# Decode attention over 65536 keys: keys transposed in place, one value tile split unevenly over its partitions, scores copied in pairs, one store for seven heads

## The chip, the core and the metric

The kernel runs on one core of one Trainium2 chip. The metric is the device time of one execution in microseconds (us); the time of a kernel is the median of its runs. A profile is one further execution with the hardware profiler on; its instructions cover a span that is a little shorter than the execution's time.

## The reference

One query token with 32 heads attends to 65536 keys. Eight key-value heads serve four query heads each; a head is 128 wide. All data are bf16.

```
B, Hq, Hkv, Sq, Sk, D = 1, 32, 8, 1, 65536, 128
q: (B, Hq, Sq, D)   k, v: (B, Hkv, Sk, D)

k = jnp.repeat(k, rep, axis=1); v = jnp.repeat(v, rep, axis=1)      # rep = 4
scores = jnp.einsum("bhqd,bhkd->bhqk", q, k) * D ** -0.5
p = softmax(scores, axis=-1)
return jnp.einsum("bhqk,bhkd->bhqd", p, v)
```

Keys and values are 268 MB and each of them is used once.

## The kernel before, in words

A key-value head ("group" g, eight of them) has its 65536 rows laid over 128 partitions, 512 rows each. The rows come in four tiles s = 0..3 of 128 rows per partition: 128 x 128 x 128 bf16, 4 MB in one transfer, 32 KB for each partition. Key tiles `kn` and value tiles `vb` share one pool of four buffers (`iopool`, tag "io"). All loads go through the queue of SyncE (SP) in program order: while group g's keys are loaded, the values of group g-1 are loaded between them, so that from the second group on the order is k(g,0), v(g-1,0), k(g,1), v(g-1,1) and so on, and the last four loads are v(7,0) to v(7,3). A load is issued when its buffer is free.

`k_step` takes a key tile. The contraction runs over the head's 128 dimensions, so they have to be on partitions: VectorE transposes 32 x 32 blocks of bf16 pairs taken as fp32, two of the eight row classes w at a time, from `kn` into a tile `T` (pool `tpool`, three buffers). That is four transposes of 128 x 2048 fp32 for each key tile (L135). TensorE then does four matmuls for each w (L144), all 32 of a tile summed in one PSUM bank `sc` (three buffers); `wq` holds the queries, shifted so that each w writes rows of its own. ScalarE copies `sc` to its quarter of `S_g` (L151).

After four tiles `softmax` finds the maximum (VectorE, TensorE), and ScalarE computes the exponentials with their sums (`E_g`, L177). `transpose_weights` (L190) turns them for use as weights; it is placed in the middle of the first key tile of the next group.

`v_stream` multiplies a value tile by the weights with 32 matmuls (L213) into `psum_o`, `pick` masks and adds four parts (L224, L230), and `finish` divides by the sums and calls `store`, which writes heads 0 to 3 during group 4's pass and heads 4 to 6 during group 7's (L250, on ScalarE's queue).

The last tile v(7,3) is loaded in pieces of 64, 32, 16, 8, 4 and 4 rows. `finish_last` streams the first 64 rows like every tile, and takes the rest in an order written out by hand (`manual_schedule`): transposed matmuls for rows 64 to 119 (L290), the part from `pick` in between (L287), single rows 120 to 123 (L280), a transpose (L297), single rows 124 to 127, then two VectorE operations and the store of head 7 (L305).

Everything else is ordered by the framework, which sets the semaphores. Transfers of SP's and ScalarE's queues take eight completion semaphores in turn, so a transfer's issue waits until the eighth transfer before it has landed.

Of the kernel before, what the change touches and what calls it, by code (L numbers as in the profile page):

```python
# [8 lines left out]
ALU = mybir.AluOpType  # L9
# [3 lines left out]

NT = 128
NW = 16

LATE = (64, 120, 124)

# [2 lines left out]
def kernel(  # L21
# [17 lines left out]
    nc = tc.nc  # L39
    P = nc.NUM_PARTITIONS  # L40
    B, Hq, Sq, D = q.shape
    _, Hkv, Sk, _ = k.shape
    assert B == 1 and Sq == 1 and D == P
    HPG = Hq // Hkv
    assert HPG == 4 and HPG * Hkv == Hq
    R = Sk // P
    KT = R // NT
    W = NT // NW
    assert W * HPG == 32 and KT == 4
    SCALE = float(D) ** -0.5  # L50

    fp32 = mybir.dt.float32
    bf16 = mybir.dt.bfloat16

    const = ctx.enter_context(tc.tile_pool(name="const", bufs=1))
    iopool = ctx.enter_context(tc.tile_pool(name="iopool", bufs=4))
    tpool = ctx.enter_context(tc.tile_pool(name="tpool", bufs=3))
    spool = ctx.enter_context(tc.tile_pool(name="spool", bufs=2))
    epool = ctx.enter_context(tc.tile_pool(name="epool", bufs=2))
    opool = ctx.enter_context(tc.tile_pool(name="opool", bufs=2))  # L60
    stats = ctx.enter_context(tc.tile_pool(name="stats", bufs=2))
    psc = ctx.enter_context(tc.tile_pool(name="psc", bufs=3, space=bass.MemoryType.PSUM))
    psm = ctx.enter_context(tc.tile_pool(name="psm", bufs=1, space=bass.MemoryType.PSUM))
    psf = ctx.enter_context(tc.tile_pool(name="psf", bufs=1, space=bass.MemoryType.PSUM))
    pso = ctx.enter_context(tc.tile_pool(name="pso", bufs=2, space=bass.MemoryType.PSUM))
# [9 lines left out]
    for x in range(2):  # L75
# [8 lines left out]
        out=sel[:, :], in_=ident[:, :].rearrange("p (x h) -> p h x", h=HPG), axis=AX.X, op=ALU.max  # L84
# [3 lines left out]
        out=blk[:, :], in_=ident[:, :].rearrange("p (j w h) -> p w j h", w=W, h=HPG), axis=AX.XY, op=ALU.max  # L88
# [6 lines left out]
    nc.gpsimd.memset(one[:, :], 1.0)  # L95
    lsum_all = const.tile([P, Hkv], fp32)
    o_all = const.tile([P, Hkv, D], fp32)

    qx = const.tile([P, D], bf16)
    nc.vector.transpose(out=qx[:, :].bitcast(fp32), in_=qn[:, :].bitcast(fp32))  # L100
# [3 lines left out]
    def queries(g):  # L104
        eng = nc.vector if g == 0 else nc.gpsimd
        wv = Wq[g % 2][:, :].rearrange("p (b r x) -> p b r x", b=2, r=2)
        for a in range(4):
            qd = slice(32 * a, 32 * a + 32)
            eng.tensor_copy(  # L109
                out=wv[qd, :, :, 32 * a + 28:32 * a + 28 + HPG],  # L110
                in_=qv[qd, :, :, g * HPG:(g + 1) * HPG],
            )

    queries(0)

    S_tiles, E_tiles, ET_tiles, o_tiles = {}, {}, {}, {}

    def k_load(g, s):
        kn = iopool.tile([P, NT, D], bf16, name="kn", tag="io", align_bytes=2048)
        src = k[0, g].rearrange("(p n) d -> p n d", p=P)  # L120
        nc.sync.dma_start(out=kn[:, :, :], in_=src[:, s * NT:(s + 1) * NT, :])
        return kn

    def k_step(g, s, kn):
        if s == 0:
            S_tiles[g] = spool.tile([P, KT, 4 * P], fp32, name="S_g")
        wq = Wq[g % 2]
        kv = kn[:, :, :].rearrange("p (c w) d -> p w c d", w=W)
        sc = psc.tile([P, 4 * P], fp32, name="sc")
        for w in range(W):  # L130
            if s == 0 and w == W // 2 and g > 0:
                transpose_weights(g - 1)
            if w % 2 == 0:
                T = tpool.tile([P, 2, NW, D], bf16, name="T")
                nc.vector.transpose(  # L135
                    out=T[:, :, :, :].bitcast(fp32),
                    in_=kv[:, w:w + 2].bitcast(fp32),
                )
            Tv = T[:, w % 2].rearrange("p n (b i r) -> p n b i r", b=2, r=2)
            for b in range(2):  # L140
                for r in range(2):
                    bp = 2 * b + r
                    at = bp * WX + 28 - 4 * w
                    nc.tensor.matmul(  # L144
                        out=sc[:, :],
                        lhsT=wq[:, at:at + P],
                        rhs=Tv[:, :, b, :, r],
                        start=(w == 0 and bp == 0),
                        stop=(w == W - 1 and bp == 3),
                    )  # L150
        nc.scalar.copy(out=S_tiles[g][:, s, :], in_=sc[:, :])  # L151

    def softmax(g):
        S_g = S_tiles[g]
# [32 lines left out]
    def transpose_weights(g):  # L187

        ET = epool.tile([P, KT, NW, 32], bf16, name="ET")
        nc.vector.transpose(  # L190
            out=ET[:, :, :, :].rearrange("p s c x -> p (s c x)"),
            in_=E_tiles[g][:, :, :].rearrange("p s x -> p (s x)"),
        )
        ET_tiles[g] = ET

    def v_load(g, s, pieces=(NT,)):
        vb = iopool.tile([P, NT, D], bf16, name="vb", tag="io", align_bytes=2048)
        src = v[0, g].rearrange("(p n) d -> p n d", p=P)
        x = 0
        for step in pieces:  # L200
            n0 = s * NT + x
            nc.sync.dma_start(out=vb[:, x:x + step, :], in_=src[:, n0:n0 + step, :])  # L202
            x += step
        return vb

    def v_stream(g, s, vb, rows, last):

        if s == 0:
            o_tiles[g] = pso.tile([P, 4, D], fp32, name="psum_o")
        for c in range(rows // W):  # L210
            for x in range(2):
                j = 2 * x + c % 2
                nc.tensor.matmul(  # L213
                    out=o_tiles[g][32 * j:32 * j + 32, :, :],
                    lhsT=ET_tiles[g][:, s, c, :],
                    rhs=vb[:, c * W + 4 * x:c * W + 4 * x + 4, :],
                    start=(s == 0 and c < 2),
                    stop=(last and c >= rows // W - 2),
                )

    def pick(g):

        o_m = opool.tile([P, 4, D], fp32, name="o_m")
        nc.vector.tensor_tensor(  # L224
            out=o_m[:, :, :],
            in0=o_tiles[g][:, :, :],
            in1=mask[:, :].unsqueeze(2).broadcast_to([P, 4, D]),
            op=ALU.mult,
        )
        nc.vector.tensor_reduce(  # L230
            out=o_all[:, g, :], in_=o_m[:, :, :].rearrange("p x d -> p d x"), axis=AX.X, op=ALU.add
        )

    def sums(g0, n):

        psum_l = psm.tile([HPG, n], fp32, name="psum_l", tag="misc")
        nc.tensor.matmul(out=psum_l[:, :], lhsT=sel[:, :], rhs=lsum_all[:, g0:g0 + n], start=True, stop=True)  # L237
        rl = stats.tile([HPG, n], fp32, name="rl")
        nc.vector.reciprocal(out=rl[:, :], in_=psum_l[:, :])
        return rl  # L240

    def store(g0, n, psum_f, rl):
        o_out = stats.tile([HPG, n, D], bf16, name="o_out")
        nc.vector.tensor_tensor(  # L244
            out=o_out[:, :, :],
            in0=psum_f[:, :, :],
            in1=rl[:, :].unsqueeze(2).broadcast_to([HPG, n, D]),
            op=ALU.mult,
        )
        nc.scalar.dma_start(  # L250
            out=out[0, :, 0, :].rearrange("(g h) d -> h g d", h=HPG)[:, g0:g0 + n, :], in_=o_out[:, :, :]
        )

    def finish(g0, n):
        rl = sums(g0, n)
        psum_f = psf.tile([HPG, n, D], fp32, name="psum_f", tag="fin")
        nc.tensor.matmul(  # L257
            out=psum_f[:, :, :], lhsT=sel[:, :], rhs=o_all[:, g0:g0 + n, :], start=True, stop=True
        )
        store(g0, n, psum_f, rl)  # L260

    def finish_last(g, s, vb):

# [43 lines left out]
    for g in range(Hkv + 1):  # L307
        if 0 < g < Hkv:
            queries(g)
        for s in range(KT):  # L310
            if g < Hkv:
                k_step(g, s, k_load(g, s))
            elif s == 0:
                transpose_weights(g - 1)
            if g > 0:
                last = s == KT - 1
                if g == Hkv and last:
                    finish_last(g - 1, s, v_load(g - 1, s, pieces=(64, 32, 16, 8, 4, 4)))
                else:
                    v_stream(g - 1, s, v_load(g - 1, s), NT, last)  # L320
                    if last:
                        pick(g - 1)
                    if last and g % 4 == 0:
                        finish(g - 4, 4)
                    if last and g == Hkv - 1:
                        finish(g - g % 4, g % 4)
        if g < Hkv:
            softmax(g)

# [29 lines left out]
```

## Time and profile before

| | |
|---|---|
| median of 3 runs | 632.34 us (631.98 to 632.54) |
| the profiled execution | 631.69 us, its span 629.6 us |
| DMA | 268.78 MB, mean 427 GB/s |
| PE busy | 363.2 us (58%) |
| DVE busy | 340.4 us (54%) |
| ACT busy | 36.8 us (6%) |
| K tile load, issue to landing | 29.6 us (median of 32) |
| V tile load, issue to landing | 34.1 us (median of 31) |

Times in the profile are us from the start of the span unless marked ns. PE is TensorE's matmul, PEld its weight load, DVE is VectorE, ACT ScalarE, POOL GpSimd, SP SyncE; a "q" behind an engine's name is its sequencer. L135 is line 135 of the kernel before. The DMA work of the core is done by 16 DMA engines; "DMA share" is the mean busy share of these. "A <- B" in a list of waits reads: A waited for B. "x4" is a count of instructions.

### The profile page before, as it was taken

Reading aid. Unit: us, or ns where it says so; the run is one execution under the profiler, and the core shown is the slowest. Engines: PE = TensorE matmul, PEld = TensorE weight load, DVE = VectorE, ACT = ScalarE, POOL = GpSimd, SP = SyncE. Lnnn points to the kernel's source line nnn. Section 1 sums busy time; section 2 is a strip of 40 time slices with the busy share of each in tenths; the row PEclk is TensorE's granted clock in tenths of the full one; section 3 lists DMA queues with packets and bytes.
Section 4 is the critical chain, followed back from the end, with each engine's and each line's share of the span. In section 5 each row is a group of like instructions: output and inputs, shape, how many; then the busy total and the mean of one; then the engine's idle time right before and its main releaser. Section 6 shows DMA issues by size and latency. Waiting matters only on the chain.

```text
span 629.6 us, 4872 instructions
## 1 busy us (share of the span) xinstructions
PE 363.2 (58%) x2133; PEld 141.5 (22%) x2133; DVE 340.4 (54%) x201; ACT 36.8 (6%) x49; POOL 6.4 (1%) x37
## 2 busy tenths in 40 slices
PE   0686836745557554575645856447665466644645
PEld 0232312211222221222211222112221122211212
DVE  0998833774337753377543775436754366553511
ACT  0000100010000100001000010001000010000100
POOL 0000000000000000000000000000000000000000
PEclk9998988767887677876778867788677787767856
DMA  8999999999999999999999999999999999999996
GB/s 369 433 434 431 433 432 434 432 433 433 432 433 432 433 433 432 433 432 433 432 433 433 430 434 434 433 432 433 435 432 433 432 433 433 432 433 434 431 430 267
DMA packets 10192, 268.78 MB, mean 427 GB/s; under 512 B 1340, under 2 KB 1596, under 8 KB 1852
## 3 DMA queue, kind: packets, MB, share of 16 engines
q1 hardware_dynamic: 9936, 268.44, 99.0%
q8 instruction: 16, 0.26, 0.1%
q10 hardware_dynamic: 236, 0.04, 0.0%
q14 instruction: 4, 0.03, 0.0%
HBM read 268.47 MB, written 0.01 MB: 426 GB/s over the span
## 4 chain that ended last, share of the span: by engine, by line
DMA 73%; DVE 12%; issue 11%; PE 2%; ACTq 0%; DVEq 0%; SPq 0%
DMA kn<-in_k_dram 66%; DVE T L135 12%; DMA vb<-in_v_dram 5%; DMA qn<-in_q_dram 2%; PE sc L144 2%; PE psum_o L213 0%; PE psum_oT L290 0%; ACTq L70 0%; PE psum_f L280 0%; DVEq L135 0%; DVE wq L109 0%; PE psum_f L287 0%; DVE sel L83 0%; DVE o_last L302 0%; SPq L202 0%
## 5 line engine op out<-in xcount | busy, mean ns | idle before, releaser
L144 PE MATMUL sc<-T,wq 128*128 128x512 bf16 x1024 | 287.9, 445 | 220.2 <-DVE T L135 220.2
L135 DVE STREAM_TRANSPOSE T<-kn 128x2048 f32<-128x2048 f32 x128 | 284.2, 2277 | 198.6 <-DMA kn<-in_k_dram 198.6
L144 PEld LDWEIGHTS <-wq 128*128 128x128 bf16 x1024 | 109.5, 109 | 394.6 <-issue 159.5
L213 PE MATMUL psum_o<-vb,ET 128*32 128x512 bf16 x1008 | 65.1, 403 | 12.0 <-DMA vb<-in_v_dram 9.8
L151 ACT COPY S_g<-sc 128x512 f32<-128x512 f32 x32 | 18.8, 587 | 510.8 <-PE sc L144 510.8
L213 PEld LDWEIGHTS <-ET 128*32 128x32 bf16 x1008 | 25.5, 100 | 49.2 <-issue 28.3
L156 DVE TENSOR_REDUCE mx<-S_g 128x1 f32<-128x2048 f32 x8 | 18.3, 2286 | 26.1 <-ACT S_g L151 26.1
L190 DVE STREAM_TRANSPOSE ET<-E_g 128x2048 bf16<-128x2048 bf16 x8 | 18.5, 2311 | 16.3 <-ACT E_g L177 16.3
L177 ACT ACTIVATE E_g<-S_g,nmb 128x2048 bf16<-128x2048 f32 x8 | 16.0, 2001 | 47.6 <-DVE nmb L174 40.4
L224 DVE TENSOR_TENSOR o_m<-psum_o,mask 128x512 f32<-128x512 f32 x8 | 5.5, 682 | 21.5 <-PE psum_o L213 21.5
L109 POOL COPY wq<-qx 32x16 bf16<-32x16 bf16 x28 | 5.3, 190 | 426.9 <-PE sc L144 410.2
L160 PE MATMUL psum_t<-ident,mx 128*1 128x128 f32 x8 | 2.2, 270 | 11.2 <-DVE mx L156 11.2
L100 DVE STREAM_TRANSPOSE qx<-qn 128x64 f32<-128x64 f32 x1 | 0.2, 245 | 15.0 <-DMA qn<-in_q_dram 15.0
L172 PE MATMUL psum_b<-one,mrow 1*128 1x1 f32 x16 | 3.5, 288 | 8.3 <-DVE mrow L166 8.3
L230 DVE TENSOR_REDUCE o_all<-o_m 128x128 f32<-128x512 f32 x8 | 8.0, 1000 | 0.0
L172 PEld LDWEIGHTS psum_b<-one,mrow 1*128 1x128 f32 x16 | 3.0, 232 | 12.2 <-issue 11.4
L237 PE MATMUL psum_l<-lsum_all,sel 128*4 128x4 f32 (+2 forms) x6 | 0.6, 166 | 7.7 <-ACT E_g L177 7.7
L257 PE MATMUL psum_f<-o_all,sel 128*4 128x512 f32 (+1 forms) x4 | 2.6, 730 | 2.9 <-DVE o_all L230 2.9
L160 PEld LDWEIGHTS psum_t<-ident,mx 128*1 128x1 f32 x8 | 0.6, 79 | 15.1 <-DVE mx L156 11.6
L174 DVE COPY nmb<-psum_b 128x1 f32<-128x1 f32 x8 | 1.2, 152 | 2.9 <-PE psum_b L172 2.9
L290 PE MATMUL psum_oT<-ET,vb 128*128 128x4 bf16 x56 | 1.8, 167 | 1.4 <-DMA vb<-in_v_dram 1.4
L244 DVE TENSOR_TENSOR o_out<-psum_f,rl 4x512 bf16<-4x512 f32 (+1 forms) x2 | 1.2, 612 | 2.5 <-PE psum_f L257 2.5
(30 smaller groups left out, 16.1 us busy)
## 6 DMA issues: line engine op xcount, KB each, us to landing
kn<-in_k_dram SPq DMA_DIRECT2D x32, 4096.0 KB, 29.6
vb<-in_v_dram SPq DMA_DIRECT2D x31, 4096.0 KB, 34.1
vb<-in_v_dram SPq DMA_DIRECT2D x1, 2048.0 KB, 29.5
vb<-in_v_dram SPq DMA_DIRECT2D x1, 1024.0 KB, 31.6
vb<-in_v_dram SPq DMA_DIRECT2D x1, 512.0 KB, 32.3
vb<-in_v_dram SPq DMA_DIRECT2D x1, 256.0 KB, 32.5
vb<-in_v_dram SPq DMA_DIRECT2D x2, 128.0 KB
qn<-in_q_dram ACTq DMA_DIRECT2D x4, 8.0 KB, 10.1
```

What stands on the lines that cost most here:

```text
L109: eng.tensor_copy(out=wv[qd, :, :, 32 * a + 28:32 * a + 28 + HPG], in_=qv[qd, :, :, g * HPG:(g + 1) * HPG],)
L135: nc.vector.transpose(out=T[:, :, :, :].bitcast(fp32), in_=kv[:, w:w + 2].bitcast(fp32),)
L144: nc.tensor.matmul(out=sc[:, :], lhsT=wq[:, at:at + P], rhs=Tv[:, :, b, :, r], start=(w == 0 and bp == 0), stop=(w == W - 1 and bp == 3),)
L151: nc.scalar.copy(out=S_tiles[g][:, s, :], in_=sc[:, :])
L156: nc.vector.tensor_reduce(out=mx[:, :], in_=S_g[:, :, :].rearrange("p n c -> p (n c)"), axis=AX.X, op=ALU.max)
L160: nc.tensor.transpose(out=psum_t[:, :], in_=mx[:, :], identity=ident[:, :])
L172: nc.tensor.matmul(out=psum_b[:, :], lhsT=mrow[:, :], rhs=one[:, :], start=True, stop=True)
L177: nc.scalar.activation(out=E_g[:, :, :].rearrange("p s x -> p (s x)"), in_=S_g[:, :, :].rearrange("p s x -> p (s x)"), func=ACT.Exp, bias= ...
L190: nc.vector.transpose(out=ET[:, :, :, :].rearrange("p s c x -> p (s c x)"), in_=E_tiles[g][:, :, :].rearrange("p s x -> p (s x)"),)
L213: nc.tensor.matmul(out=o_tiles[g][32 * j:32 * j + 32, :, :], lhsT=ET_tiles[g][:, s, c, :], rhs=vb[:, c * W + 4 * x:c * W + 4 * x + 4, :], ...
L224: nc.vector.tensor_tensor(out=o_m[:, :, :], in0=o_tiles[g][:, :, :], in1=mask[:, :].unsqueeze(2).broadcast_to([P, 4, D]), op=ALU.mult,)
L230: nc.vector.tensor_reduce(out=o_all[:, g, :], in_=o_m[:, :, :].rearrange("p x d -> p d x"), axis=AX.X, op=ALU.add)
```

## The change

Four edits.

- `T` and its pool are gone. Each transpose takes four row classes at a time and writes them back over the key tile itself; the matmuls read the key tile. A key tile has two transposes of 128 x 4096 fp32 where it had four of 128 x 2048.
- `sc` is a tile of two PSUM banks for two key tiles, with two buffers. ScalarE copies both banks at once at every second key tile.
- `o_out` is one tile for heads 0 to 6, written by `finish` in two parts, and stored by one transfer during group 7's pass.
- The value tile v(7,2), the last but one, is loaded in six transfers where it was one: rows 0 to 79 of all 128 partitions, then rows 80 to 127 of partitions 0 to 111, and the same rows of partitions 112 to 115, 116 to 119, 120 to 123 and 124 to 127.

```
+FEW = 48
...
-    tpool = ctx.enter_context(tc.tile_pool(name="tpool", bufs=3))
...
-    psc = ctx.enter_context(tc.tile_pool(name="psc", bufs=3, space=bass.MemoryType.PSUM))
+    psc = ctx.enter_context(tc.tile_pool(name="psc", bufs=2, space=bass.MemoryType.PSUM))
...
+    o_out = const.tile([HPG, Hkv - 1, D], bf16)
...
-        sc = psc.tile([P, 4 * P], fp32, name="sc")
+        if s % 2 == 0:
+            sc_tiles[g] = psc.tile([P, 2, 4 * P], fp32, name="sc")
+        sc = sc_tiles[g][:, s % 2, :]
         for w in range(W):
             if s == 0 and w == W // 2 and g > 0:
                 transpose_weights(g - 1)
-            if w % 2 == 0:
-                T = tpool.tile([P, 2, NW, D], bf16, name="T")
-                nc.vector.transpose(
-                    out=T[:, :, :, :].bitcast(fp32),
-                    in_=kv[:, w:w + 2].bitcast(fp32),
-                )
-            Tv = T[:, w % 2].rearrange("p n (b i r) -> p n b i r", b=2, r=2)
+            if w % 4 == 0:
+                groups = kv[:, w:w + 4].bitcast(fp32)
+                nc.vector.transpose(out=groups, in_=groups)
+            Tv = kv[:, w].rearrange("p n (b i r) -> p n b i r", b=2, r=2)
...
-        nc.scalar.copy(out=S_tiles[g][:, s, :], in_=sc[:, :])
+        if s % 2 == 1:
+            nc.scalar.copy(out=S_tiles[g][:, s - 1:s + 1, :], in_=sc_tiles[g][:, :, :])
...
+        if few:
+            n0 = s * NT + x
+            p0 = 0
+            for p1 in (112, 116, 120, 124, P):
+                nc.sync.dma_start(out=vb[p0:p1, x:, :], in_=src[p0:p1, n0:n0 + few, :])
+                p0 = p1
...
-        store(g0, n, psum_f, rl)
+        nc.vector.tensor_tensor(
+            out=o_out[:, g0:g0 + n, :],
+            in0=psum_f[:, :, :],
+            in1=rl[:, :].unsqueeze(2).broadcast_to([HPG, n, D]),
+            op=ALU.mult,
+        )
...
-                    v_stream(g - 1, s, v_load(g - 1, s), NT, last)
+                    few = FEW if g == Hkv and s == KT - 2 else 0
+                    v_stream(g - 1, s, v_load(g - 1, s, pieces=(NT - few,), few=few), NT, last)
...
                     if last and g == Hkv - 1:
                         finish(g - g % 4, g % 4)
+                        nc.scalar.dma_start(
+                            out=out[0, 0:g * HPG, 0, :].rearrange("(g h) d -> h g d", h=HPG), in_=o_out[:, :, :]
+                        )
```

More of the change, by code (lines that the diff above doesn't have):

```diff
@@ L114 @@
     queries(0)
-    S_tiles, E_tiles, ET_tiles, o_tiles = {}, {}, {}, {}
+    S_tiles, sc_tiles, E_tiles, ET_tiles, o_tiles = {}, {}, {}, {}, {}
     def k_load(g, s):
@@ L144, in k_step @@
                     nc.tensor.matmul(
-                        out=sc[:, :],
+                        out=sc,
                         lhsT=wq[:, at:at + P],
@@ L194, in transpose_weights, with v_load @@
         ET_tiles[g] = ET
-    def v_load(g, s, pieces=(NT,)):
+    def v_load(g, s, pieces=(NT,), few=0):
         vb = iopool.tile([P, NT, D], bf16, name="vb", tag="io", align_bytes=2048)
@@ L240, in sums @@
         return rl
[L242 to L252, printed above, removed]
     def finish(g0, n):
```

## The prediction

> **What bounds the kernel now.** I read the page's second part first, then the chain of waits, then the waits of SP's own queue, then the tail.
>
> ```profile
> span 629.6 us, 4872 instructions
> ...
> GB/s 369 433 434 431 433 432 434 432 433 433 432 433 432 433 433 432 433 432 433 432 433 433 430 434 434 433 432 433 435 432 433 432 433 433 432 433 434 431 430 267
> ...
> q8 instruction: 16, 0.26, 0.1%
> ...
> DMA 73%; DVE 12%; issue 11%; PE 2%; ACTq 0%; DVEq 0%; SPq 0%
> ...
> kn<-in_k_dram SPq DMA_DIRECT2D x32, 4096.0 KB, 29.6
> ```
>
> Bytes flow at 430 to 435 GB/s in every slice but the first and the last. 268.4 MB at 433 GB/s is 620 us, so only some 10 us of the span are not transfer. A 4 MB load takes 4.194 MB / 433 GB/s = 9.7 us and lands 29.6 us after its issue, so about two further loads (20 us) stand queued. The 12% of DVE in the chain are therefore no bound: a buffer freed some us later leaves the queue shorter and the stream whole.
>
> ```profile
> SPq L121 <- DVE T L135: 273.7, 28, 14.2
> SPq L121 <- DMA kn<-in_k_dram: 130.0, 25, 10.1
> SPq L202 <- PE psum_o L213: 108.4, 28, 5.0
> ...
> SPq L202 <- DMA out_dram<-o_out: 7.0, 1, 7.0
> ```
>
> SP waits for transposes to free key buffers and for matmuls to free value buffers; once, 7.0 us, for a store. What can move the time is the end, where the windows show this (columns: stretch, length, busy time and count of PE, PEld, DVE, ACT, POOL, then clock, DMA share, GB/s):
>
> ```profile
> 618.00:622.00 4.00, 2.44 (x32) 0.85 (x24) 0.06 (x1) 0.00 (x0) 0.00 (x0) 0.87 0.97 408
> 622.00:623.00 1.00, 0.00 (x0) 0.00 (x0) 0.97 (x2) 0.00 (x0) 0.00 (x0) 0.72 0.84 327
> 623.00:624.00 1.00, 0.69 (x26) 0.70 (x27) 0.70 (x1) 0.00 (x0) 0.00 (x0) 0.50 0.58 232
> 624.00:625.00 1.00, 1.00 (x23) 0.56 (x20) 0.00 (x0) 0.00 (x0) 0.00 (x0) 0.50 0.53 198
> 625.00:626.00 1.00, 1.00 (x26) 0.78 (x22) 0.16 (x1) 0.00 (x0) 0.00 (x0) 0.50 0.18 63
> ```
>
> The DMA share falls to 0.5 for the last 2.7 us: about half of the 16 engines are done 3 us before the others. From 622 to the last landing at 625.8 the shares add up to 0.84 + 0.58 + 0.53 + 0.18 = 2.13 us of full work in 3.8, so evening out the engines perfectly is worth 1.6 us at most.
>
> The packet records of the trace say why. Each engine carries eight 32 KB packets per load (1213 ns each, back to back). The 16 instruction fetches of the quoted q8 row, 16 KB each, hold one engine up by 1.42 us apiece and come round to the same eight engines: two each, 2.84 us. For a late full load the 16 engines' completions stand at 0 to 0.25 us (five), 0.64, 0.70, 1.87, and 2.73 to 3.09 (eight), counted from the first. The store of `o_out`, whose slow side is 4 long, ran on four engines; they stand at 0.21, 0.22, 0.70 and 1.87. None belongs to the late eight; the one at 1.87 was held up by two 8 KB fetches (at 95.9 and 349.6 us, 0.84 us each), the one at 0.70 by one at 593.2.
>
> **The tile v(7,2), part by part.** Packet medians are 46 ns for 1 KB, 84 for 2, 159 for 4, 309 for 8, 611 for 16: straight, so a 12 KB packet (48 rows) costs 0.46 us and a 20 KB one (80 rows) 0.76. Before, an engine has 8 x 1.21 = 9.7 us of this tile. After, if the 112 partitions spread evenly, 12 engines have 8 x 0.76 + 7 x 0.46 = 9.3, and the four that take the 4-partition transfers have 4 x 0.46 = 1.84 more, 11.1. So twelve engines gain about 0.42 us and four lose 1.44. The late eight then end at 3.09 - 0.42 = 2.67. The four end at 0.21 + 1.44 = 1.65 twice, 0.70 + 1.44 = 2.14 and 1.87 + 1.44 = 3.31.
>
> That last engine decides the sign of the small term. Its hold-ups fall where VectorE's instruction count has reached 66 and 185 (300 at the third), so they are VectorE's code. The change takes 64 transposes and most of the 104 semaphore instructions beside them out of VectorE's 315, leaving about 150: one fetch, not three. The engine then ends at 3.31 - 0.84 = 2.47, ahead of the late eight, and the end moves by **-0.42 us**. If it keeps both, 3.31 - 3.09 = **+0.2 us**. I take -0.42.
>
> Nothing behind hides that gain: the 32-row piece's landing starts PE at 623.31, PE is then busy to 626.9 and the store follows, so the chain moves with the landings.
>
> What the edit costs if four engines writing to four neighbouring partitions hinder each other is not in the trace. The bounds: none (0.46 us per packet), or the four take turns, 4 x 4 x 0.46 = 7.3 us instead of 1.84, which puts those engines 5.5 us later, and the end at 1.65 + 5.5 - 3.1 = +4 to, for the latest of them, +5 us. The nearest row: the four query loads put 32 partitions on 16 engines beside the full key stream, and their 256 B packets took 18 ns where the straight line above gives 17.5. I take none.
>
> [...]
>
> **Keys in place.** 64 transposes go. From 64 elements in 245 ns (L100) and 2048 in 2277, one of 4096 costs 4.4 us, 64 of them 280 us against 284: nothing, and off the bound. But the key buffer is now freed by PE.
>
> ```profile
> 324.21 8.89 DVE L135 STREAM_TRANSPOSE T<-kn 128x2048 f32<-128x2048 f32 x4 [10.43 <-DMA kn<-in_k_dram]
> 326.57 9.92 PE L144 MATMUL sc<-T,wq 128*128 128x512 bf16 x32 [8.13 <-DVE T L135]
> 333.13 0.33 SPq L121 DMA_DIRECT2D kn<-in_k_dram  x1
> ```
>
> After, PE starts at 324.2 + 4.4 = 328.6. A stretch of these matmuls begins at 0.43 us each for about 12, then goes at 0.24 (the timeline at 579.8), so 32 take 6.1 + 3.8 = 9.9 and end at 338.5; the buffer is free 5.4 us later than 333.1. That is issued ahead: the shortest lead of any load over the moment the first engine wants it is 12.5 us, typically 14 to 18. Queued behind on SP is the next value load, with 19 or more. Cost 0; without that cover, 5.4 us once per tile that runs dry.
>
> **Copies in pairs.** 16 of 128 x 1024: from 587 ns for 512 and 2001 for 2048, 1.06 us, so the softmax starts 0.5 us later, plus 2.3 us for PE's later end (2.1 us late start, DVE no longer pacing). Hidden: the weights of group 7, ready at 600.4, come at 603.2, with PE waiting for v(7,1) until 606.3.
>
> **One store.** The store at 361.9 goes; the other has 7 packets per engine instead of 3. On SP it matters: the eight completion semaphores go round, and the 7.0 us wait above is the last piece waiting for that store's semaphore. With five more transfers the turn falls on the *first* 64-row piece, and all six pieces queue behind it on SP. Before, the store was issued at 595.55 and had landed by 603.95. After: issued 2.8 us later, 598.4; its packets go one between two 32 KB packets, four more are 4 x 1.22 = 4.9; landed at 598.4 + 8.4 + 4.9 = 611.7. The piece's packets start 1.0 us after its issue (first key load: 0.74 to 1.75), 612.8. The late eight finish v(7,2) from 614.8 on, so 2 us are to spare, the early ones idle for under 1 us, which they have.
>
> **Sum.** 629.6 - 0.42 = 629.2 for the span, 2.1 us outside it as before. The profiled execution lies 0.65 us under the median, so on the median 632.34 - 0.42 = 631.9.
>
> **Rivals.** (1) Slower: the four 4-partition transfers take turns, +4 to +5 us, 636 to 637; with partial sharing less. It decides once those engines lose more than 1.0 us (2.67 - 1.65) over their plain 1.84. For it: nothing here proves them free; against: the 18 ns row. 0.18. (2) The store's wait: if the softmax chain comes over 2 us later than worked out, every further us is one; 632.5 to 634. 0.08. (3) The key tile's second transpose waits for the matmuls that read the first half, since both now touch one tile: 4.4 + 6.1 + 4.4 + 3.8 = 18.7 us plus 1.9 for values against 19.4 between key tiles, 1.2 us for each of 28 tiles less the 12 us of lead, some +20 us. The row classes are disjoint, so 0.04. (4) The change doesn't do what it says: the slow engine keeps its hold-ups, 632.5, inside "same"; part of the forecast's case. (5) The fetches shift too and the engines even out: up to -1.6, 630.7. 0.06.
>
> **How the numbers follow.** The forecast's case has 0.63, with 631.3 to 632.8 of its own (-0.42 or +0.2, and the runs' spread of 0.3). About 0.2%, 1.26 us, is what a measurement of this kernel can tell from no change. Same: 0.63 plus the smaller half of (2), 0.67. Slower: (1), (3), the other half of (2) and 0.01 unnamed, 0.27. Faster: (5), 0.06. The range takes in (5) partly, (2), and the lower part of (1): 631.1 to 635.5.
>
> **What would show it.** Right: GB/s of 430 to 435 in all middle slices; an SP wait for `o_out` of over 10 us in the tail; 12 KB transfers landing within 2.5 us of each other; the last stretch shorter by 0.4 us with a higher DMA share. Wrong: DMA share near 0.3 with four engines working at the end (1), a gap in the DMA share near 613 (2), a dip in the middle slices (3).

## The result, and the profile after

The changed kernel takes **638.98 us** (median of 5 runs, 638.56 to 639.69) against 632.17 us for the kernel before beside it (5 runs, 631.98 to 632.54): a ratio of 1.0109 with a 95% interval of 1.0094 to 1.0124, or 6.8 us slower. The forecast was 631.9 us, with a range from 631.1 to 635.5. The profiled execution took 639.69 us, its span 636.6.

First the page after. The second part gives GB/s by slices of a fortieth of the span, the third the DMA queues, the fourth the chain, the fifth the groups (busy time, mean ns), the sixth the transfers.

```profile
span 636.6 us, 4719 instructions
...
GB/s 373 449 432 427 428 427 430 440 439 435 428 428 428 432 437 443 430 427 430 427 436 439 434 434 427 430 429 436 434 433 436 427 430 433 434 432 437 429 249 249
...
q14 instruction: 2, 0.02, 0.0%
...
DMA 62%; PE 22%; DVE 15%; issue 0%; ACTq 0%; ACT 0%; DVEq 0%; SPq 0%
...
L139 DVE STREAM_TRANSPOSE kn<-kn 128x4096 f32<-128x4096 f32 x64 | 280.2, 4418 | 186.4 <-DMA kn<-in_k_dram 186.4
...
L153 ACT COPY S_g<-sc 128x1024 f32<-128x1024 f32 x16 | 16.2, 1013 | 517.5 <-PE sc L145 517.5
...
kn<-in_k_dram SPq DMA_DIRECT2D x32, 4096.0 KB, 23.7
```

The middle slices run at 427 to 449 GB/s, less evenly than before (430 to 435) and at the same mean of 433: nothing is lost in the first 600 us. The last but one slice falls from 430 to 249. Windows of 4 us show where (length, then busy time and count of PE, PEld, DVE, ACT and POOL, then granted clock, DMA share, GB/s):

```profile
602.00:606.00 4.00, 2.67 (x28) 1.06 (x32) 1.31 (x2) 0.00 (x0) 0.00 (x0) 0.50 1.00 428
606.00:610.00 4.00, 2.45 (x44) 1.05 (x37) 0.00 (x0) 0.00 (x0) 0.00 (x0) 0.95 1.02 388
610.00:614.00 4.00, 0.00 (x0) 0.00 (x0) 0.00 (x0) 0.00 (x0) 0.00 (x0) 0.90 0.98 204
614.00:618.00 4.00, 1.72 (x20) 0.67 (x19) 0.00 (x0) 0.00 (x0) 0.00 (x0) 0.50 1.04 192
618.00:622.00 4.00, 0.61 (x8) 0.00 (x0) 0.00 (x0) 0.00 (x0) 0.00 (x0) 0.50 1.02 190
622.00:626.00 4.00, 1.47 (x12) 0.45 (x13) 0.00 (x0) 0.00 (x0) 0.00 (x0) 0.50 0.93 389
...
629.00:630.00 1.00, 0.74 (x8) 0.00 (x0) 0.21 (x1) 0.00 (x0) 0.00 (x0) 0.50 0.84 337
630.00:631.00 1.00, 0.73 (x27) 0.73 (x28) 0.97 (x2) 0.00 (x0) 0.00 (x0) 0.50 0.75 290
631.00:632.00 1.00, 0.68 (x13) 0.29 (x10) 0.55 (x1) 0.00 (x0) 0.00 (x0) 0.50 0.55 197
632.00:633.00 1.00, 1.00 (x27) 0.87 (x27) 0.04 (x1) 0.00 (x0) 0.00 (x0) 0.50 0.05 17
```

For 12 us, from 610 to 622, the DMA share is 0.98 to 1.04 and the rate is 190 to 204 GB/s. The engines are busy all the time and move half as much. This is the stretch in which the last 48 rows of v(7,2) arrive: the four transfers of 4 partitions have landed at 619.7, 621.0, 622.0 and 622.7, and the one over 112 partitions, issued before them, lands last, at 623.2. TensorE waits for it and goes on at 623.28. In the packet records a 12 KB packet, worked out at 0.46 us, has a median of 0.945 us (0.46 to 1.73), and 20 KB packets of the 80-row transfer, which take 0.761 us undisturbed, go up to 2.23 us.

The very end is hardly evener. From 629 the shares are 0.84, 0.75, 0.55 and 0.05, that is 2.19 us of full work up to the last landing at 632.7; from 622 before, they are 0.84, 0.58, 0.53 and 0.18, or 2.13 us up to 625.8. So 1.5 us are lost where 1.7 were, and the engines finish the last piece 3.2 us apart where it was 3.0.

The chain of waits after names a store, and SP's waits agree:

```profile
591.05 1.02 ACT S_g L153
...
596.14 1.45 PE psum_f L254 x2
...
598.20 9.75 DMA out_dram<-o_out
...
608.01 19.78 DMA vb<-in_v_dram
...
627.84 1.92 PE psum_o L222 x16
```

```profile
SPq L205 <- DMA out_dram<-o_out: 11.0, 1, 11.0
```

The 64-row piece is issued when the store has landed, at 608.01, and takes 19.78 us. The chain reads as if the store were to blame. Whether it is, is the question of the third experiment below.

### The profile page after: what moved, and what is told of

Its sections match the earlier page's. It is cut to its first block, busy times and chain, and to the rows that moved or that the text cites. A ratio compares the mean times of both kernels' runs of the same rounds, so it can differ in the third digit from the quotient of the medians.

```text
span 636.6 us, 4719 instructions
## 1 busy us (share of the span) xinstructions
PE 361.9 (57%) x2133; PEld 142.3 (22%) x2133; DVE 336.9 (53%) x137; ACT 34.2 (5%) x33; POOL 6.5 (1%) x37
## 4 chain that ended last, share of the span: by engine, by line
DMA 62%; PE 22%; DVE 15%; issue 0%; ACTq 0%; ACT 0%; DVEq 0%; SPq 0%
DMA kn<-in_k_dram 55%; PE sc L145 21%; DVE kn L139 14%; DMA vb<-in_v_dram 3%; DMA qn<-in_q_dram 2%; DMA out_dram<-o_out 2%; DVE mx L158 0%; DVE o_all L239 0%; PE psum_o L222 0%; PE psum_f L254 0%; DVE o_m L233 0%; ACTq L71 0%; PE psum_f L282 0%; ACT S_g L153 0%; PE psum_oT L292 0%
## 5 line engine op out<-in xcount | busy, mean ns | idle before, releaser
L145 PE MATMUL sc<-kn,wq 128*128 128x512 bf16 x1024 | 287.2, 446 | 220.7 <-DVE kn L139 201.2
L139 DVE STREAM_TRANSPOSE kn<-kn 128x4096 f32<-128x4096 f32 x64 | 280.2, 4418 | 186.4 <-DMA kn<-in_k_dram 186.4
L153 ACT COPY S_g<-sc 128x1024 f32<-128x1024 f32 x16 | 16.2, 1013 | 517.5 <-PE sc L145 517.5
## 6 DMA issues: line engine op xcount, KB each, us to landing
kn<-in_k_dram SPq DMA_DIRECT2D x32, 4096.0 KB, 23.7
```

Of the source, the lines that this page charges most:

```text
L139: nc.vector.transpose(out=groups, in_=groups)
L145: nc.tensor.matmul(out=sc, lhsT=wq[:, at:at + P], rhs=Tv[:, :, b, :, r], start=(w == 0 and bp == 0), stop=(w == W - 1 and bp == 3),)
L153: nc.scalar.copy(out=S_tiles[g][:, s - 1:s + 1, :], in_=sc_tiles[g][:, :, :])
```

## The experiments

Four edits were made at once, and the fourth has two features: more transfers, and transfers over fewer than 128 partitions. The theory was that the partition sets are the cost; the rivals were the other three edits, and the store's semaphore with the longer queue behind it.

**Without the uneven split.** Only the split of v(7,2) is undone.

```
-FEW = 48
+FEW = 0
```

> The changed kernel with v(7,2) loaded in one transfer again (FEW = 0); the other three edits stay. Theory A (the 112- and 4-partition transfers are what is slow: between 608 and 622 us of the changed kernel's trace the DMA moves 190 GB/s with all engines busy): within 0.5 us of the kernel before, 631.9 to 632.7, and the SP wait for the store's semaphore falls on a later piece without harm. Theory B (the store's semaphore now met earlier in SP's order starves the queue): also near 632, since the turn moves back. Theory C (keys in place: the key buffers freed later by PE cost leads): still some 636 to 639, with GB/s dips in the middle slices. Separates C from A and B.

Measured: 632.10 us against 631.97, ratio 1.0005 (0.9997 to 1.0014).

```profile
610.00:614.00 4.00, 0.00 (x0) 0.00 (x0) 0.00 (x0) 0.00 (x0) 0.00 (x0) 0.76 0.93 397
614.00:618.00 4.00, 1.71 (x20) 0.73 (x23) 0.00 (x0) 0.00 (x0) 0.00 (x0) 0.50 0.96 410
618.00:622.00 4.00, 2.32 (x36) 0.93 (x28) 0.00 (x0) 0.00 (x0) 0.00 (x0) 0.89 0.99 417
```

The hole is gone, and keys in place, copies in pairs and one store together cost nothing that can be measured. Its size accounts for the loss: in these 12 us the changed kernel moved (397 - 204 + 410 - 192 + 417 - 190) GB/s x 4 us = 2.55 MB less, which at 427 GB/s takes 6.0 us of the 6.8 by which the spans differ (636.6 and 629.8).

**The uneven split alone.** The kernel before, with the six transfers of v(7,2).

```
...
+            for p1 in (112, 116, 120, 124, P):
+                nc.sync.dma_start(out=vb[p0:p1, x:, :], in_=src[p0:p1, n0:n0 + few, :])
...
```

> The kernel before with the six transfers of v(7,2) alone added; keys, copies and stores as before. Theory A: the whole loss, +6 to +7.5 us, 638 to 640. Theory B: less, since here the store has 3 packets per engine and is issued earlier, +0 to +3. Theory C: 632 to 633.

Measured: 639.58 us, ratio 1.0119 (1.0105 to 1.0132). The split alone makes the whole loss, with no store of seven heads and no transposes in place.

```profile
610.00:614.00 4.00, 0.00 (x0) 0.00 (x0) 0.00 (x0) 0.00 (x0) 0.00 (x0) 0.82 0.96 197
614.00:618.00 4.00, 1.81 (x20) 0.69 (x19) 0.00 (x0) 0.00 (x0) 0.00 (x0) 0.50 1.03 188
```

**Six transfers, all over 128 partitions.** The same count of transfers and the same turn of the completion semaphores.

```
-                    v_stream(g - 1, s, v_load(g - 1, s, pieces=(NT - few,), few=few), NT, last)
+                    v_stream(g - 1, s, v_load(g - 1, s, pieces=(80, 12, 9, 9, 9, 9) if few else (NT,)), NT, last)
```

> The changed kernel with v(7,2) in six transfers still, but each over all 128 partitions: rows 80, 12, 9, 9, 9, 9. Same number of transfers, same turn of the semaphores, same wait of SP for the store; only the sets of partitions differ. Theory A: 632 to 633, every packet at the price of its size (9 rows: about 0.09 us). Theory B: the loss stays, 636 to 639.

Measured: 632.24 us, ratio 1.0005 (0.9996 to 1.0014). First its windows, then SP's waits:

```profile
610.00:614.00 4.00, 1.10 (x16) 0.42 (x15) 0.00 (x0) 0.00 (x0) 0.00 (x0) 0.80 1.02 408
614.00:618.00 4.00, 2.87 (x28) 0.93 (x21) 0.00 (x0) 0.00 (x0) 0.00 (x0) 0.78 1.05 439
```

```profile
SPq L205 <- DMA out_dram<-o_out: 11.1, 1, 11.1
```

SP waits as long for the store as in the changed kernel (11.1 us against 11.0), and it costs nothing: the queue holds enough. The chain was right that the piece was issued behind the store, and wrong as a cause. All 20 KB packets take 0.761 us, all 2.25 KB packets 0.093, and 125 of the 128 packets of 3 KB 0.121; the other three, just behind an instruction fetch of 16 KB, go up to 0.33. No packet is stretched as in the split.

**Is it the four transfers of 4 partitions?** They become one of 16.

```
-            for p1 in (112, 116, 120, 124, P):
+            for p1 in (112, P):
```

> The changed kernel with rows 80 to 127 in two transfers, of 112 and of 16 partitions. Theory A with the 4-partition transfers as the slow part (four engines on four neighbours, as the prediction priced it): the four engines are relieved, +0 to +1.5 us, 632 to 634. Theory A with the 112-partition transfer as the slow part: most of the loss stays, +4 to +7 us, 636 to 639, with 12 KB packets near 0.95 us in the first of the two.

Measured: 639.03 us, ratio 1.0115 (1.010 to 1.013).

```profile
610.00:614.00 4.00, 0.00 (x0) 0.00 (x0) 0.00 (x0) 0.00 (x0) 0.00 (x0) 0.78 0.91 184
614.00:618.00 4.00, 2.21 (x20) 0.67 (x19) 0.00 (x0) 0.00 (x0) 0.00 (x0) 0.50 1.07 221
618.00:622.00 4.00, 0.11 (x4) 0.00 (x0) 0.00 (x0) 0.00 (x0) 0.00 (x0) 0.50 1.07 227
```

The same hole without a transfer of 4 partitions. The suspect is now the transfer over 112, which the forecast had taken as plain; the one of 16 partitions beside it is not ruled out by this run.

**The 112-partition transfer by itself.** From here on the base is the kernel without the split (632.10 us), and an extra load into a tile that nothing reads follows v(7,2). One load has 48 rows of 112 partitions, the other 42 rows of 128: 1.376 MB both. The kernel before took 631.84 to 632.15 us beside these and the later runs, and 631.97 beside the base, so differences under 0.3 us mean nothing here.

```
+nc.sync.dma_start(out=xb[0:112, :, :], in_=src[0:112, n0:n0 + 48, :])
...
+nc.sync.dma_start(out=xb[:, 0:42, :], in_=src[:, n0:n0 + 42, :])
```

> The kernel of e1 with one transfer more, behind v(7,2): 48 rows of 112 partitions, 1.376 MB, into a tile that nothing reads. At full rate, 433 GB/s, it costs 3.2 us: 635.3. If the shape of 112 partitions is what is slow (theory A), 12 KB packets near 0.9 us instead of 0.46 and some 4 to 8 us on top: 639 to 644. If only a value tile that the kernel waits for is hurt, 635 to 636.

> The same extra bytes, 1.376 MB, in the usual shape: 42 rows of all 128 partitions. All theories: +3.2 us, 635.0 to 635.8, with 10.5 KB packets at 0.40 us. The control for e5.

Measured: 641.89 us (ratio 1.0159, 1.0144 to 1.0174) over 112 partitions and 635.40 us (1.0062, 1.0047 to 1.0077) over 128. The first windows are of the load over 112, the second of that over 128:

```profile
616.00:619.00 3.00, 0.00 (x0) 0.00 (x0) 0.00 (x0) 0.00 (x0) 0.00 (x0) 0.50 0.70 143
619.00:622.00 3.00, 2.54 (x25) 1.05 (x28) 0.00 (x0) 0.00 (x0) 0.00 (x0) 0.50 1.06 223
```

```profile
616.00:619.00 3.00, 2.92 (x28) 1.25 (x31) 0.00 (x0) 0.00 (x0) 0.00 (x0) 0.50 1.03 441
619.00:622.00 3.00, 0.69 (x8) 0.15 (x1) 0.00 (x0) 0.00 (x0) 0.00 (x0) 0.79 0.97 415
```

The same bytes cost 641.89 - 632.10 = 9.8 us over 112 partitions and 635.40 - 632.10 = 3.3 over 128; 1.376 MB at 427 GB/s is 3.2 us. So 112 partitions cost 6.5 us more. The 10.5 KB packets of the full load all took 0.404 us; the 12 KB packets had a median of 0.916, and 32 KB packets of v(7,2) that were still running went up to 3.17 us (1.21 is their median, 1.76 the longest at the end of the kernel before).

**Reading side or writing side?** The same two loads with a source that is one contiguous stretch.

```
-src = v[0, g].rearrange("(p n) d -> p n d", p=P)
+src = v[0, g, 0:112 * 48].rearrange("(p n) d -> p n d", p=112)
```

> As e5, the same 112 partitions of the same tile written, but read from one stretch of memory without gaps instead of 12 KB pieces 128 KB apart. If the loss is on the writing side (several engines at one part of SBUF at a time), it stays as in e5, 639 to 644. If it is on the reading side (the order in which the engines walk through the memory), it goes: 635 to 636.

> As e6, all 128 partitions written, read from one stretch without gaps. The control for e7: 635.0 to 635.8 if such a stretch is read at full rate; slower says that e7 can't separate the two sides.

Measured: 642.61 us (1.0168, 1.0151 to 1.0185) and 635.41 us (1.0057, 1.0042 to 1.0072). Packet medians are 0.912 and 0.404 us, as with the rows far apart. Where it is read from plays no part that can be seen.

**Four transfers of 4 partitions, together and apart.** Both read the same rows and move 196 KB; only the partitions that they write to differ: 0 to 3, 4 to 7, 8 to 11 and 12 to 15, or four that lie four apart (0, 4, 8, 12, and so on).

```
 for i in range(4):
-    nc.sync.dma_start(out=xb[4 * i:4 * i + 4, :, :], in_=src[4 * i:4 * i + 4, n0:n0 + 48, :])
+    nc.sync.dma_start(out=xb[i:16:4, :, :], in_=src[4 * i:4 * i + 4, n0:n0 + 48, :])
```

> The kernel of e1 with four transfers more behind v(7,2), into a tile that nothing reads: 48 rows of partitions 0 to 3, 4 to 7, 8 to 11, 12 to 15. Four engines get 4 x 12 KB each. If four engines that write to four neighbours take turns (the prediction's first rival), their packets take up to 4 x 0.46 = 1.84 us, 7.3 us in all instead of 1.84, of which the engines' early finish hides some 3: +2 to +4 us, 634 to 636. If they don't hinder each other: 0.46 us a packet and no more time, 632.0 to 632.5, as three of these engines are done 2 us before the last.

> The same rows of memory read in the same order by the same engines, but written to partitions 0, 4, 8, 12, then 1, 5, 9, 13 and so on. If partitions four apart have write paths of their own: 0.46 us a packet and 632.0 to 632.5. If any transfer over so few partitions is slow: like e8, 634 to 636.

Measured: 632.94 us (1.0019, 1.0009 to 1.0028) together and 631.99 us (1.0005, 0.9995 to 1.0014) apart. Together lies between the two cases that were expected: the four are not free, and they do not take turns in full. The first window is that of the transfers together, the second of those apart:

```profile
612.00:616.00 4.00, 0.00 (x0) 0.00 (x0) 0.00 (x0) 0.00 (x0) 0.00 (x0) 0.50 0.93 271
```

```profile
612.00:616.00 4.00, 0.00 (x0) 0.00 (x0) 0.00 (x0) 0.00 (x0) 0.00 (x0) 0.73 0.91 389
```

Together, the sixteen 12 KB packets have a median of 0.85 us; apart, each of them takes 0.460, the price of the straight line. With the source equal, the destination alone decides. That places the cost on the writing side.

**How few partitions?** The load of the same bytes over 96 and over 64 partitions.

```
+nc.sync.dma_start(out=xb[0:96, 0:56, :], in_=src[0:96, n0:n0 + 56, :])
...
+nc.sync.dma_start(out=xb[0:64, 0:84, :], in_=src[0:64, n0:n0 + 84, :])
```

> As e5 with the same 1.376 MB as 56 rows of 96 partitions. If every set short of 128 runs the 16 engines at about half rate, as 112 partitions do: packets of 14 KB near 1.05 us instead of 0.53 and 639 to 643. If 96, three full blocks of 32, keep clear of the collisions: 635.3 to 637.

> As e5 with the same 1.376 MB as 84 rows of 64 partitions. If half of the partitions have half of the write paths: 16 engines at 217 GB/s, 6.4 us instead of 3.2, packets of 21 KB near 1.6 us instead of 0.79, 638 to 640. If the loss of 112 comes from its odd number of 7 per engine alone: 635 to 636.

Measured: 642.38 us (1.0168, 1.0153 to 1.0183) and 641.97 us (1.016, 1.0145 to 1.0176). With the 641.89 of 112 partitions this is one price: 9.8 to 10.3 us for 1.376 MB, whether 16, 32 or 64 partitions are left out. The lower rate expected for 64 partitions, with 638 to 640 us, fell short of it by 2 us: two windows of that run have 208 and 199 GB/s (619 to 625, shares 0.99 and 0.95), but as a whole its 1.376 MB took 9.9 us, 139 GB/s.

**The strided sets at the partitions that the change uses.** If sets four apart are free, the uneven split could be had with them. The two kernels repeat the comparison at partitions 112 to 127.

```
-    nc.sync.dma_start(out=xb[112 + 4 * i:116 + 4 * i, :, :], in_=src[112 + 4 * i:116 + 4 * i, n0:n0 + 48, :])
+    nc.sync.dma_start(out=xb[112 + i:128:4, :, :], in_=src[112 + 4 * i:116 + 4 * i, n0:n0 + 48, :])
```

> [...] If only neighbours collide: 0.46 us a packet, 631.9 to 632.4, as e9. If an engine that writes where another engine streams collides with it: 12 KB packets of 0.7 us and more, 32 and 16 KB packets of other engines stretched too, 632.6 to 634.

> The four 4-partition transfers of the change, partitions 112 to 115, 116 to 119, 120 to 123, 124 to 127, as extra ones beside the usual load. As e8 if it is the neighbours that count: 632.6 to 633.7, all packets stretched for some 4 us. It sizes what these four transfers alone cost in the change: about 1 us of its 7.

Measured: 634.22 us (1.0032, 1.002 to 1.0044) apart, 635.21 us (1.0049, 1.0037 to 1.0062) together, both above what was expected. Apart first, then together; without the transfers the rate of this window is 393 GB/s:

```profile
612.00:616.00 4.00, 0.00 (x0) 0.00 (x0) 0.00 (x0) 0.00 (x0) 0.00 (x0) 0.79 1.06 281
```

```profile
612.00:616.00 4.00, 0.00 (x0) 0.00 (x0) 0.00 (x0) 0.00 (x0) 0.00 (x0) 0.54 0.91 167
```

Being four apart is not what makes a set free. At 0 to 15 it was (0.460 us for a packet); at 112 to 127 the packets have a median of 0.902 us apart and 1.189 together, and 196 KB cost 2.1 and 3.1 us over the kernel without them, when at 427 GB/s they take 0.46. Meanwhile 32 KB packets take up to 3.5 us (together). In the trace of the change each of these transfers lands in four parts, the one over 112 partitions in 16, and the four follow one another (616.93 to 619.71, 618.37 to 621.0, 619.11 to 621.97, 620.8 to 622.72): read as four engines that carry all four in turn. More than four engines are slowed: twelve undisturbed ones would move 12/16 x 427 = 320 GB/s alone, and the window has 167. The landings say the same. In the run with the sets together, eight engines finish v(7,2) at 619.2 to 619.4, where they were done at 615.8 to 616.3 without the four transfers. If an engine takes its queue in order, as the packet records of the kernel before, followed from end to start, show it (eight of 32 KB, then eight of 16, then eight of 8), they are not the four that carry these: the first of the four transfers, queued behind v(7,2), had landed by 616.5.

**What the runs show, and what stays open.** Shown: the loss is the partition sets of v(7,2), on their writing side, and the transfer over 112 partitions is enough for it: by itself it costs 6.5 us more than its bytes over 128 partitions, against a loss of 6.8 in the change. The four transfers of 4 partitions by themselves cost 2.6 us more than theirs (635.21 - 632.10 - 0.46), so the two prices do not add up in the change; how they overlap there is not shown. Packets of the full loads and of the short sets are in flight together: in the change the 12 KB packets run from 608.95 to 622.24, the last 20 KB packet ends at 614.54, and the 16 KB packets of the 64-row piece start at 614.86. Why a short set is slow is not shown: the trace does not record which engine wrote to which partition, so the runs give its price and not its cause. For the same reason it is not shown why four partitions four apart are free at 0 to 15 (0.460 us) and not at 112 to 127 (0.902). It also stays open why engines that carry only full-load packets are slowed too, and why the cost is the same for 112, 96 and 64 partitions.

## Why the prediction was wrong

**What bounds the kernel: right.** Bytes at a constant rate decide until 610 us, and only the end moved.

**The step that failed** is the price of the split: "I take none", and ahead of it "if the 112 partitions spread evenly, 12 engines have 8 x 0.76 + 7 x 0.46 = 9.3". Its terms of 0.46 us measured 0.945 (median), and its 0.76 up to 2.23 us. It failed in two ways. The doubt was put only on the four transfers of 4 partitions; one transfer of 16 instead of them lost as much (ratio 1.0115), and a 112-partition load by itself costs 6.5 us more than its bytes. For the four transfers too "none" was wrong: at the same partitions they cost 3.1 us by themselves, with 1.189 us for a 12 KB packet. And the cost was kept to the four engines concerned, hence "+4 to +5" as the upper end; the rate of the whole core halved (190 to 204 GB/s where 397 to 417 were moved without the split), and it was 6.8. The row that decided, 18 ns for 256 B packets of the query loads, was no witness: 32 KB went by in all, and packets of 12 KB, 48 times as large, were judged by it. The straight line from 1 to 16 KB was no witness for it either, since all its packets came from transfers over 128 partitions. The even spread of the 112 partitions over the engines was the author's assumption, and no run shows it; the trace after shows that this transfer lands in 16 parts (615.60 to 623.24) and each of those over 4 in four.

**Rival (1)** had the right sign and kind, four transfers that are slower where they write side by side (0.85 us for a packet at partitions 0 to 15, 0.460 apart), and with "partial sharing" it holds for the four transfers by themselves. But its place was too narrow, and its sign in the profile did not come: it expected a DMA share near 0.3 with four engines working at the end, and the share stays near 1 while the GB/s halve. The sign of being right, 12 KB transfers that land within 2.5 us of each other, did not come either: their last landings go from 619.7 to 623.2.

**The gain of 0.42 us** (0.40 by its own terms, 9.7 - 9.3) came at most in small part. The step on VectorE's code was right: the q14 row went from 4 instruction packets to 2. But the evening out was to come from the uneven split, and the last stretch lost 1.5 us instead of 1.7, in one profile of each kernel. Where two of the four fetches are gone and v(7,2) is whole (632.10 against 631.97) nothing moves, as by the prediction's account, in which the late eight set the end there.

**Keys in place: right.** 64 transposes at 4418 ns (worked out: 4.4 us) keep VectorE busy for 280.2 us (280). The timeline of the same key tile:

```profile
324.27 8.77 DVE L139 STREAM_TRANSPOSE kn<-kn 128x4096 f32<-128x4096 f32 x2 [10.64 <-DMA kn<-in_k_dram]
328.76 9.33 PE L145 MATMUL sc<-kn,wq 128*128 128x512 bf16 x32 [8.78 <-DVE kn L139]
...
338.13 0.33 SPq L123 DMA_DIRECT2D kn<-in_k_dram  x1
```

The two transposes run back to back, so rival (3), a transpose that waits for the matmuls, is out. The matmuls take 9.33 us (9.9), and the next load is issued at 338.13 (338.5), 5 us later than before. That is the fall from 29.6 to 23.7 us from issue to landing, and it costs nothing since the queue stays full.

**Copies in pairs: right**, 1013 ns (1.06 us) each, and hidden.

**The store: right in its working, better in its size.** It was issued at 598.20 (598.4) and SP waited 11.0 us for it (over 10). It landed at 607.95, not 611.7: its packets now pass between 20 KB packets of 0.76 us, not 32 KB ones of 1.21. Rival (2) is out by the six full transfers, where the same wait costs nothing.

## What to carry to other kernels

Load over all 128 partitions, and split a tile by rows and not by partitions when transfers must be evened out or moved: here, beside full loads, the same bytes cost three times as much over 112 partitions as over 128. Balance that is worth tenths of a microsecond is no reason to leave the one shape whose packets the traces have shown to be undisturbed (with six full transfers all 20 KB packets took 0.761 us). When a DMA-bound kernel slows, look at the GB/s beside the DMA share: here a share of 1.02 stood beside 190 GB/s in the change, and one of 1.05 beside 439 with six full transfers.

## What was unexpected of the hardware

- A transfer over 112 partitions in the midst of full loads halves the whole core's rate: 223 GB/s at a share near 1 when it comes by itself, against 415 for the same bytes over 128; 190 to 204 in the change, against 397 to 417. 96 and 64 partitions cost the same to 0.5 us.
- Packets of the full loads are slowed with it: 20 KB packets of 0.76 us take up to 2.23, and 32 KB packets of 1.21 us up to 3.17. Four transfers of 4 partitions stretch them up to 3.5, and the rate of 167 GB/s shows that engines which carry none of the four are slowed as well.
- Four partitions four apart are free at 0 to 15 (0.460 us for each 12 KB packet) and not at 112 to 127 (0.902).
- SP can wait 11 us for a store's semaphore at no cost: 11.1 us with six full transfers, at a ratio of 1.0005. In the change, where the chain of waits runs through that store, the wait was 11.0.
